# Small loads one per unit, and a rebuilt prologue with DMA transposes, in an attention and MLP kernel on one core

## Chip, core and metric

The kernel runs on one core of one Trainium2 chip. The metric is the time on the device in microseconds (us). The kernel before takes 1110.81 us (median of 3 runs, 1109.93 to 1113.89; with the fourth run, 1110.77). A "ratio" is the mean time of one kernel's runs over that of the kernel before in the same rounds, so it is not quite the ratio of the medians quoted beside it.

## The reference, cut to what matters

```python
xn = _layernorm(A_x)                       # 2048 x 1024, bf16
s = attention(xn, A_wqkv, A_wo)            # 32 heads of 32
h = gelu(layernorm(xn) @ w1 + b1)          # 1024 -> 3584
g = silu(h @ w2 + b2)                      # 3584 -> 1024
return A_x + s * g
```

## The kernel before

The program is straight-line code. A small scheduler on the host fixes the order of each engine's instructions. The attention runs in 512 "units" (8 head groups of 4 heads, 8 query blocks, 8 key pairs). Each unit has three parts:

- scores on TensorE (8 matmuls),
- two exps of 128x1024 on ScalarE,
- probabilities times V, with row sums, on TensorE ("PV", 16 matmuls).

Between scores and PV TensorE gets one "item" of other work, named by a letter of the plan. `a` is an MLP first layer item, `w` a second layer item, `q` a Q or K projection of later heads, `v` a V projection, `o` an output projection, and `.` is nothing. The first 8 units are the prologue. They make x normalised and transposed (`xnT`) and the first heads' Q, K and V, and have no items.

```python
def transp(tb):                      # 8 transposes of 128x128 on TensorE ...
    op("tensor", f, r=[("xnb", i), "ident"], w=[("b", bk)])
    op("scalar", copy of 128x1024 from PSUM to xnT[:, :, tb])     # ... and a copy on ScalarE
def mm4(e, outs, lhs, rhs, start, stop):      # one matmul as four tiles of 32 columns
    for j in range(4):
        e.matmul(outs(j), lhsT=lhs(j), rhs=rhs, tile_position=(0, 32 * j), ...)
def pair_kq(p):                      # mm4 for K, then Q: 64 matmuls; pair_v: 64 for V
    ...
def pro_unit(p):
    norm_pair(p + 1)                 # VectorE: statistics and x normalised, two tiles
    if p < 3: ynorm(p)               # VectorE: second normalisation, stored to DRAM
    if 0 < p < NP - 1: transp_pair(p + 1)
    pair_kq(p); pair_v(p)
    if p == 0: transp_pair(1)
# loads: wq 512 KB each, yTc one DMA transpose of 352x1024, wo one load of 2 MB,
# biases element by element:
op("gpsimd", lambda e: e.dma_start(b1T[:], B_b1.rearrange("(fb p) -> p fb", p=128)), ...)
... (cut)
```

All loads but those of the biases are issued by SyncE, in order. The MLP weights come in 336 loads of 256 KB.

The softmax here doesn't subtract the row's maximum and nothing guards it: scores larger than these inputs give would overflow.

Of the kernel before, what the change touches and what calls it, by code (L numbers as in the profile page):

```python
# [13 lines left out]
a v a a a q a q a v a v a a a q a a v a q a a v q a a v a a q a q a a v q a q a a a q q v a a q w3 w4 w3 w4 v w4 w2 w2 w2 a a v a q v v a q q a a a a a q a q a a q a a v a q a q q a a a v v a a a q v a a a a q q a a w3 v w3 w4 w4 w4 q v q v w2 v q w3 w3 a a a v v q a a a q a a q q a a a q q a v a q a v a a q a q a a a a v a a q a q v v v a a q q q v a q q a w3 q v q w5 q w4 w3 q w3 w4 w2 w4 a a a v v a a q a a q a q q v a a q a q v a q a a a a q a a a q a a v a a a a v a v a q a v q q w3 w4 v q w4 w4 w4 v w4 w3 w4 a a a q q a a a a v a v a a a a a v q a a v a a a q a a a v a a q q v a q q a a q a q q q a v w3 v w4 w4 q w4 w4 w4 w4 w4 a a a a q q a a q a a q a a a q a q q a a a a a a a a a a q q a a a a a q a q w2 w4 w3 w4 w2 w3 w5 o o o o o o o o o o o o w4 o o o o o o o o o o o o o o o o o o o o o o o o o o o . o o o o o o o . o o  # L14
# [153 lines left out]
def bass_recurrent_scan__mha_block__mixer_channel_mlp__prompt_kernel(  # L168
# [32 lines left out]
    t0 = 0  # L201
# [9 lines left out]
    with ExitStack() as st:  # L211
# [30 lines left out]
        gst = [sb(f"gst{i}", [128, CW], BF16) for i in range(2)]  # L242
        b1T = sb("b1T", [128, FB], F32)
# [10 lines left out]
        xnb = [hflat[:, i * D:(i + 1) * D] for i in range(4)]  # L254
# [23 lines left out]
        def load_wq(hp, which=(0, 1, 2)):  # L278
            for t3 in which:
                src = A_wqkv[:, t3 * D + hp * 256:t3 * D + (hp + 1) * 256].rearrange("(c p) n -> p c n", p=128)  # L280
                op("sync", lambda e, src=src, t3=t3: e.dma_start(wq[:, t3, :, :], src), w=[("wq", t3)], dma=f"wq{t3}", c=512)

        for tb in range(4):
            load_x(tb)
            if tb in (1, 3):
                load_wq(0, (1 if tb == 1 else 0,))
        load_x(4)
        load_x(5)
        load_wq(0, (2,))
        for tb in range(6, NT):  # L290
            load_x(tb)
# [4 lines left out]
        op("gpsimd", lambda e: e.dma_start(b1T[:], B_b1.rearrange("(fb p) -> p fb", p=128)), w=["b1"], dma="b1", c=256)  # L296
        op("gpsimd", lambda e: e.dma_start(b2h[:], B_b2.rearrange("(nb p) -> p nb", p=128)), w=["b2"], dma="b2", c=64)


# [8 lines left out]
        def rstd(b):  # L308
            lo, hi = 2 * b, 2 * b + 2
            L = lambda k: lnp[:, k, lo:hi]  # L310
            mvk = [("mv", t) for t in range(lo, hi)]
            op("vector", lambda e: e.tensor_scalar_add(L(0), mv[:, lo:hi, 1], EPS), r=mvk, w=[("l0", b)], c=169.0)
            op("gpsimd", lambda e: e.tensor_tensor(L(2), L(0), mhalf[:, 0:2], op=ALU.pow), r=[("l0", b), "mhalf"], w=[("l2", b)], c=708.0)  # L313

        def nbias(b):
            lo, hi = 2 * b, 2 * b + 2
            L = lambda k: lnp[:, k, lo:hi]
            mvk = [("mv", t) for t in range(lo, hi)]
            op("vector", lambda e: e.scalar_tensor_tensor(L(3), mv[:, lo:hi, 0], -1.0, L(2), op0=ALU.mult, op1=ALU.mult),
               r=mvk + [("l2", b)], w=[("l3", b)], c=107.0)  # L320

        def ycoef(b):
            lo, hi = 2 * b, 2 * b + 2
            L = lambda k: lnp[:, k, lo:hi]
            mvk = [("mv", t) for t in range(lo, hi)]
            op("gpsimd", lambda e: e.tensor_tensor(L(4), mv[:, lo:hi, 1], L(2), op=ALU.mult), r=mvk + [("l2", b)], w=[("l4", b)])
            op("gpsimd", lambda e: e.tensor_tensor(L(4), L(4), L(2), op=ALU.mult), r=[("l4", b), ("l2", b)], w=[("l4", b)])
            op("gpsimd", lambda e: e.tensor_scalar(L(4), L(4), 1.0, EPS, op0=ALU.mult, op1=ALU.add), r=[("l4", b)], w=[("l4", b)])
            op("gpsimd", lambda e: e.tensor_tensor(L(5), L(4), mhalf[:, 0:2], op=ALU.pow), r=[("l4", b), "mhalf"], w=[("l5", b)], c=760.0)
            op("gpsimd", lambda e: e.tensor_tensor(L(6), L(2), L(5), op=ALU.mult), r=[("l5", b), ("l2", b)], w=[("l6", b)])  # L330
            op("gpsimd", lambda e: e.tensor_tensor(L(7), L(3), L(5), op=ALU.mult), r=[("l5", b), ("l3", b)], w=[("l7", b)])

        def xnorm(tb):
            i = tb % 4
            op("vector", lambda e: e.tensor_scalar(xnb[i], xst[:, tb * D:(tb + 1) * D], lnp[:, 2, tb:tb + 1], lnp[:, 3, tb:tb + 1],  # L335
                                                   op0=ALU.mult, op1=ALU.add),
               r=[("xst", tb), ("l2", tb // 2), ("l3", tb // 2)], w=[("xnb", i)], c=545.0)
# [7 lines left out]
        pro_banks = [4, 5, 7]  # L345
        pbk = {"n": 0}
# [5 lines left out]
        def transp(tb):  # L352
            i, bk = tb % 4, pro_bank()
# [23 lines left out]
        def qk_item(hg, which, t0, n):  # L377
# [3 lines left out]
            def step(dc, bk):  # L381
                op("tensor", lambda e: mm4(e, lambda j: bankq(bk, j, 0, n),
                                           lambda j: wq[:, which, dc, co + 32 * j:co + 32 * j + 32],
                                           xnT[:, dc, t0:t0 + n], dc == 0, dc == DC - 1),
                   r=[("wq", which)] + [("xnT", t) for t in toks(t0, n)], w=[("b", bk)], c=("col", 1, n))
# [7 lines left out]
        def v_item(hp, tb):  # L393
            i2 = hp % 2

            def step(dc, bk):
                op("tensor", lambda e: mm4(e, lambda j: bankq(bk, j, 0, 256),
                                           lambda j: xnT[:, dc, tb * 128 + 32 * j:tb * 128 + 32 * j + 32],
                                           wq[:, 2, dc, :], dc == 0, dc == DC - 1),
                   r=[("wq", 2), ("xnT", tb)], w=[("b", bk)], c=("col", 1, 256))  # L400
# [77 lines left out]
        def load_y(c):  # L478
            t0, n = chunks[c]
            op("sync", lambda e: e.dma_start_transpose(yTc[:, :, 0:n], y_d[t0:t0 + n, :]),  # L480
               r=[("y", t) for t in toks(t0, n)], w=["yTc"], dma="yTc", c=1000)

        def w1_item(c, f):
# [8 lines left out]
            def step(dc, bk):  # L492
# [3 lines left out]
                   r=[("war", s, dc // 2), "yTc"], w=[("b", bk)], c=("col", 1, n))  # L496

            def fin(bk):
# [30 lines left out]
                def gate(i, xq, kq, fq):  # L529
                    op("vector", lambda e: e.scalar_tensor_tensor(hT[:, fq, 0:n], ut[:, i, 0:n], 1.0, xq[:, 0:n], op0=ALU.add, op1=ALU.mult),  # L530
                       r=[kus[i], kq], w=[("hT", fq)] + ([("xnb", i) for i in range(4)] if c == 0 else []), c=151 + 1.042 * n)
# [3 lines left out]
                if f == FB - 1 and c + 1 < NCH:  # L535
                    load_y(c + 1)
# [43 lines left out]
        def load_res(tb):  # L580
            i4 = tb % NTB
            op("sync", lambda e: e.dma_start(xres[i4], x2[tb * 128:(tb + 1) * 128, :]), w=[("xres", i4)], dma=f"rx{i4}", c=256,
               after=[tail["xfree"]])
            lo, hi = tb * 128, (tb + 1) * 128
# [5 lines left out]
        def wo_item(tb, k):  # L590
# [3 lines left out]
            def pre():  # L594
                if k == 0:
                    if tb == 0:
                        for t in range(NTB):
                            load_res(t)
                    elif tb + NTB - 1 < NT:
                        load_res(tb + NTB - 1)  # L600

            def step(hc, bk):
# [4 lines left out]
                   r=["wo", ("OT", hc, tb // 2)], w=[("b", bk)], c=("col", 1, n))  # L607

            def fin(bk):
# [5 lines left out]
                   r=[("b", bk), ("gres", i4)], w=[("ofin", f2)] + ([("wq", t) for t in range(3)] if m < 2 else []), c=165 + 1.042 * n)  # L615
# [10 lines left out]
        def pair_kq(p):  # L626
            t0, bk = 256 * p, pro_bank()

            def f(e):
                for which, off in ((1, 0), (0, 256)):  # L630
                    for dc in range(DC):
                        ins = mm4(e, lambda j: bankq(bk, j, off, off + 256), lambda j: wq[:, which, dc, 32 * j:32 * j + 32],
                                  xnT[:, dc, t0:t0 + 256], dc == 0, dc == DC - 1)
                return ins
            op("tensor", f, r=[("wq", 0), ("wq", 1), ("xnT", 2 * p), ("xnT", 2 * p + 1)], w=[("b", bk)], c=("col", 16, 256))
            for nm, dst, off in (("KT", KT, 0), ("QT", QT, 256)):
                op("scalar", lambda e, dst=dst, off=off: e.activation(dst[0][:, t0:t0 + 256], bank(bk, off, off + 256), ACT.Copy),
                   r=[("b", bk)], w=[(nm, 0, 2 * p), (nm, 0, 2 * p + 1)], c=263.0)

        def pair_v(p):  # L640
            bk = pro_bank()

            def f(e):
                for i in range(2):
                    t0 = (2 * p + i) * 128
                    for dc in range(DC):
                        ins = mm4(e, lambda j: bankq(bk, j, 256 * i, 256 * i + 256), lambda j: xnT[:, dc, t0 + 32 * j:t0 + 32 * j + 32],
                                  wq[:, 2, dc, :], dc == 0, dc == DC - 1)
                return ins
            op("tensor", f, r=[("wq", 2), ("xnT", 2 * p), ("xnT", 2 * p + 1)], w=[("b", bk)], c=("col", 16, 256))  # L650
# [3 lines left out]
        def norm_pair(p):  # L654

            more = p + 1 < NP
            if more and p >= 2:
                stat(2 * p + 2)
            nbias(p)
            xnorm(2 * p)  # L660
            xnorm(2 * p + 1)
            if more:
                if p < 2:
                    stat(2 * p + 2)
                stat(2 * p + 3)
                rstd(p + 1)
            ycoef(p)

        def transp_pair(p):
            transp(2 * p)  # L670
            transp(2 * p + 1)

        stat(0)
        stat(1)
        rstd(0)
        norm_pair(0)
        transp_pair(0)

        def pro_unit(p):
            if p + 1 < NP:  # L680
                norm_pair(p + 1)
            if p < 3:
                ynorm(p)
            if 0 < p < NP - 1:
                transp_pair(p + 1)
            pair_kq(p)
            pair_v(p)
            if p == 0:
                transp_pair(1)


# [12 lines left out]
        DU = NP  # L704
# [136 lines left out]
        while u < NU + LAG or state["qi"] < total or dq or act_tasks:  # L841
# [3 lines left out]
            elif u == NP:  # L845
# [98 lines left out]
```

## Time and profile before

| engine | busy us of 1108.7 | what it does |
|---|---|---|
| TensorE | 1082.7 | the limit over nearly the whole run |
| ScalarE | 1049.5 | exps, tanh; busy 59.9 of the 60 us from 65 to 125 us |
| VectorE | 630.4 | normalisation at first, then evictions and gelu |

First, the line of the page with each engine's busy time, share of the span and instructions.

```profile
PE 1082.7 (98%) x29952; PEld 706.5 (64%) x29952; DVE 630.4 (57%) x1415; ACT 1049.5 (95%) x1197; POOL 24.0 (2%) x64
```

Only 26 us of TensorE idle time exist. The TensorE timeline of the kernel before gives start, length, operation, count and, in brackets, the idle time before it and what ended it. In a line, `ps<-xnT,wq` names the tensor written (ps, in PSUM) and those read, `128*32` the rows and columns of the array in use, and `L366` the line of the kernel. It shows the beginning, the prologue unit 3, and the first unit after the prologue.

```profile
8.15 1.89 PE L357 MATMUL ps<-ident,hT 128*128 128x128 bf16 x16 [8.15 <-DVE hT L335]
11.50 3.61 PE L366 MATMUL ps<-xnT,wq 128*32 128x256 bf16 x64 [1.46 <-DMA wq<-in_A_wqkv_dram]
...
31.23 1.07 PE L357 MATMUL ps<-ident,hT 128*128 128x128 bf16 x16
32.23 1.93 PE L366 MATMUL ps<-xnT,wq 128*32 128x256 bf16 x64
33.99 1.92 PE L366 MATMUL ps<-wq,xnT 128*32 128x256 bf16 x64
35.84 0.40 PE L761 MATMUL ps<-QT,KT 32*128 32x256 bf16 x8
...
59.28 0.40 PE L761 MATMUL ps<-QT,KT 32*128 32x256 bf16 x8 [1.66 <-ACT P L773]
```

Differences of starts give the parts of a unit: transposes 1.00 us, K and Q 1.76, V 1.85. A unit takes 5.49 us, and nothing in it waits.

The waits of TensorE from 60 us on, in the kernel before (us in total, times, longest), are few; one of 0.2 us is left out:

```profile
PE ps L761 <- ACT P L773: 3.9, 13, 0.5
PE ps L366 <- issue: 2.9, 4, 1.4
PE ps L793 <- issue: 0.5, 1, 0.5
```

"issue" is idle time for which the profile shows no dependency. It sums to 3.4 us in five stalls. The longest is this one:

```profile
967.49 0.30 PE L366 MATMUL ps<-hT,war 128*32 128x288 bf16 x1 [1.41 <-issue]
```

### The profile page before, as it was taken

Reading aid. Unit: us, or ns where it says so; the run is one execution under the profiler, and the core shown is the slowest. Engines: PE = TensorE matmul, PEld = TensorE weight load, DVE = VectorE, ACT = ScalarE, POOL = GpSimd, SP = SyncE. Lnnn points to the kernel's source line nnn. Section 1 sums busy time; section 2 is a strip of 40 time slices with the busy share of each in tenths; the row PEclk is TensorE's granted clock in tenths of the full one; section 3 lists DMA queues with packets and bytes.
Section 4 is the critical chain, followed back from the end, with each engine's and each line's share of the span. In section 5 each row is a group of like instructions: output and inputs, shape, how many; then the busy total and the mean of one; then the engine's idle time right before and its main releaser. Section 6 shows DMA issues by size and latency. Waiting matters only on the chain.

```text
span 1108.7 us, 63340 instructions
## 1 busy us (share of the span) xinstructions
PE 1082.7 (98%) x29952; PEld 706.5 (64%) x29952; DVE 630.4 (57%) x1415; ACT 1049.5 (95%) x1197; POOL 24.0 (2%) x64
## 2 busy tenths in 40 slices
PE   6999999999999999999999999999999999999998
PEld 4866666666666666666666666666666666666665
DVE  8468762377742477652276852277743377624556
ACT  4899999899999999999999999999999999999994
POOL 4300000000000000000000000000000000000000
PEclk9999999999999999999999999999999999999999
DMA  9245255323353323333433334433234324557353
GB/s 237 71 145 174 89 146 153 114 79 108 99 150 98 89 80 114 110 87 88 130 108 92 115 76 126 144 111 108 80 104 118 111 81 144 159 155 156 96 136 108
DMA packets 202420, 129.93 MB, mean 117 GB/s; under 512 B 45488, under 2 KB 192944, under 8 KB 202160
## 3 DMA queue, kind: packets, MB, share of 16 engines
q1 hardware_dynamic: 197520, 125.86, 39.7%
q8 instruction: 234, 3.83, 1.4%
q0 software_dynamic: 4640, 0.02, 0.6%
q14 instruction: 26, 0.21, 0.1%
HBM read 104.87 MB, written 12.58 MB: 106 GB/s over the span
## 4 chain that ended last, share of the span: by engine, by line
PE 65%; ACT 32%; DVE 2%; issue 1%; DMA 0%; POOL 0%
PE ps L366 41%; ACT P L773 29%; PE ps L761 10%; PE ps L790 7%; PE ps L793 7%; ACT u L524 3%; DVE stats L303 1%; PE ps L357 1%; ACT thz L566 0%; DMA OT<-in_A_x_dram 0%; DVE hT L335 0%; DVE wq L614 0%; POOL lnp L313 0%; DVE mv L305 0%; DVE xb L507 0%
## 5 line engine op out<-in xcount | busy, mean ns | idle before, releaser
L773 ACT ACTIVATE P<-ps 128x1024 bf16<-128x1024 f32 x1024 | 970.0, 1069 | 18.1 <-PE ps L761 11.9
L793 PE MATMUL ps<-P,ones 128*32 128x256 bf16 x4096 | 257.7, 273 | 0.6 <-issue 0.5
L790 PE MATMUL ps<-P,VP 128*32 128x256 bf16 x4096 | 257.5, 273 | 0.0
L366 PE MATMUL ps<-hT,war 128*32 128x352 bf16 (+1 forms) x5376 | 226.1, 309 | 1.5 <-issue 1.4
L366 PE MATMUL ps<-yTc,war 128*32 128x352 bf16 (+1 forms) x5376 | 226.4, 309 | 0.4 <-issue 0.4
L761 PE MATMUL ps<-QT,KT 32*128 32x256 bf16 x4096 | 204.1, 273 | 7.6 <-ACT P L773 5.5
L366 PEld LDWEIGHTS ps<-hT,war 128*32 128x32 bf16 x5376 | 128.0, 96 | 76.2 <-issue 27.6
L366 PEld LDWEIGHTS ps<-yTc,war 128*32 128x32 bf16 x5376 | 127.5, 96 | 75.8 <-DVE xb L507 17.2
L562 DVE TENSOR_SCALAR zh<-ps,b2h 128x352 f32<-128x352 f32 (+1 forms) x48 | 27.5, 573 | 207.4 <-PE ps L366 207.4
L507 DVE TENSOR_SCALAR xb<-ps,b1T 128x352 f32<-128x352 f32 (+1 forms) x168 | 96.2, 573 | 78.5 <-PE ps L366 75.3
L761 PEld LDWEIGHTS ps<-QT,KT 32*128 32x128 bf16 x4096 | 61.0, 92 | 119.8 <-issue 65.7
L366 PE MATMUL ps<-xnT,wq 128*32 128x352 bf16 (+2 forms) x3200 | 130.0, 306 | 2.1 <-DMA wq<-in_A_wqkv_dram 1.5
L790 PEld LDWEIGHTS ps<-P,VP 128*32 128x32 bf16 x4096 | 110.4, 97 | 21.4 <-issue 1.7
L793 PEld LDWEIGHTS ps<-P,ones 128*32 128x32 bf16 x4096 | 110.5, 97 | 19.6 <-issue 1.1
L530 DVE SCALAR_TENSOR_TENSOR hT<-u,xb 128x352 bf16<-128x352 f32 (+1 forms) x168 | 83.8, 508 | 62.3 <-ACT u L524 62.2
L366 PEld LDWEIGHTS ps<-xnT,wq 128*32 128x32 bf16 x3200 | 77.5, 97 | 41.6 <-DVE xb L507 10.7
L517 DVE SCALAR_TENSOR_TENSOR u<-u,xb 128x352 f32<-128x352 f32 (+1 forms) x168 | 82.5, 509 | 1.9
L513 DVE TENSOR_TENSOR u<-xb 128x352 f32<-128x352 f32 (+1 forms) x168 | 82.5, 508 | 0.8
L524 ACT ACTIVATE u<-u 128x704 f32<-128x704 f32 (+1 forms) x84 | 69.9, 833 | 0.0
L366 PE MATMUL ps<-wq,xnT 128*32 128x256 bf16 x2048 | 66.6, 274 | 1.8 <-issue 1.1
L366 PE MATMUL ps<-xnT,OT 128*32 128x352 bf16 (+1 forms) x1536 | 62.9, 309 | 0.2 <-DVE wq L614 0.2
L366 PEld LDWEIGHTS ps<-wq,xnT 128*32 128x32 bf16 x2048 | 50.2, 96 | 14.0 <-DVE xb L507 5.5
(44 smaller groups left out, 435.5 us busy)
## 6 DMA issues: line engine op xcount, KB each, us to landing
war<-in_B_w_dram SPq DMA_DIRECT2D x336, 256.0 KB, 3.9
wq<-in_A_wqkv_dram SPq DMA_DIRECT2D x12, 512.0 KB, 5.3
OT<-in_A_x_dram SPq DMA_DIRECT2D x16, 256.0 KB, 7.7
y_scratch<-OT SPq DMA_DIRECT2D x16, 256.0 KB, 2.9
xnT<-in_A_x_dram SPq DMA_DIRECT2D x16, 256.0 KB, 3.8
out_dram<-wq SPq DMA_DIRECT2D x16, 256.0 KB, 2.0
gT_scratch<-gst SPq DMA_DIRECT2D x40, 88.0 KB, 1.7
xnT<-in_A_wo_dram SPq DMA_DIRECT2D x1, 2048.0 KB, 9.2
```

Source lines behind the costliest of these rows:

```text
L303: op("vector", lambda e, c=c: e.bn_stats(stats[:, tb, c, :], xt[:, c * 512:(c + 1) * 512]), r=[("xst", tb)], w=[("st", tb, c)], c=677.0)
L366: ins = e.matmul(outs(j), lhsT=lhs(j), rhs=rhs, start=start, stop=stop, tile_position=(0, 32 * j), skip_group_check=True)
L507: x0 = op("vector", lambda e: e.tensor_scalar(xb[:, 0:n], bank(bk, 0, n), b1T[:, f:f + 1], None, op0=ALU.add), r=[("b", bk), "b1"], w=[kx] ...
L513: x = op("vector", lambda e: e.tensor_tensor(ub[:, 0:n], xb[:, 0:n], xb[:, 0:n], op=ALU.mult), r=[kx], w=[ku], c=151 + 1.042 * n)
L517: x = op("vector", lambda e: e.scalar_tensor_tensor(ub[:, 0:n], ub[:, 0:n], 1.0 / 0.044715, xb[:, 0:n], op0=ALU.add, op1=ALU.mult), r=[kx, ...
L524: x = op("scalar", lambda e: e.activation(ut[:, :, 0:n], ut[:, :, 0:n], ACT.Tanh, scale=0.7978845608028654 * 0.044715), r=kus, w=kus, c=48 ...
L530: op("vector", lambda e: e.scalar_tensor_tensor(hT[:, fq, 0:n], ut[:, i, 0:n], 1.0, xq[:, 0:n], op0=ALU.add, op1=ALU.mult), r=[kus[i], kq] ...
L562: x0 = op("vector", lambda e: e.tensor_scalar(zh[:, 0:n], bank(bk, 0, n), 0.25, b2h[:, nb:nb + 1], op0=ALU.mult, op1=ALU.add), r=[("b", bk ...
L761: ins = e.matmul(bank(bks[j], kh * 256, (kh + 1) * 256), lhsT=KT[i2][32 * j:32 * j + 32, k0:k0 + 128], rhs=QT[i2][32 * j:32 * j + 32, qb * ...
L773: op("scalar", lambda e, p=p, sl=sl: e.activation(pb[:, 2 * p:2 * p + 2, :, :].rearrange("p a b q -> p (a b q)"), ps[:, sl * 1024:(sl + 1) ...
L790: e.matmul(bankq(ACC, j, 0, QW), lhsT=VP[vp][:, kb, vo + 32 * j:vo + 32 * j + 32], rhs=pb[:, j, kh, :], start=first, stop=False, tile_posi ...
L793: ins = e.matmul(bankq(ACC, j, QW, 2 * QW), lhsT=ones[:, 0:32], rhs=pb[:, j, kh, :], start=False, stop=last, tile_position=(0, 32 * j), sk ...
```

## The change

The change intends to shorten the prologue and to keep large loads from coming in bursts. Its parts:

1. x tiles 8 to 15 are transposed by DMA from SBUF, not by TensorE and ScalarE.
2. The prologue's projections are plain 128-column matmuls, not four tiles.
3. The biases come as rows, and one TensorE transpose turns them.
4. Loads at the start are reordered, tile 0 is normalised before tile 1's statistics, and three y normalisations move to ScalarE.
5. Items begin in unit 7 (`q` moves there from unit 13, which becomes `.`).
6. In the steady part wq comes in parts of 128 KB, the y transpose in four, wo in eight with the x tiles of the residual between them, about one per unit.

```diff
-a v a a a q a q a v ...
+q a v a a a . a q a v ...
+        def wq_part():
+            hp, t3, lo = wq_due.pop(0)
+            load_wq(hp, (t3,), lo, lo + 2)
-        op("gpsimd", lambda e: e.dma_start(b1T[:], B_b1.rearrange("(fb p) -> p fb", p=128)), ...)
+            op("sync", lambda e: e.dma_start(brow[0:FB, :], B_b1.rearrange("(fb p) -> fb p", p=128)), ...)
+            if tb >= TDMA:                                   # TDMA = 8
+                op("sync", lambda e: e.dma_start_transpose(xnT[:, :, tb * 128:(tb + 1) * 128], xnb[i]), ...)
+                return
-                        ins = mm4(e, lambda j: bankq(bk, j, off, off + 256), ...
+                        ins = e.matmul(bank(bk, off, off + 256), lhsT=wq[:, which, dc, 0:128], rhs=xnT[:, dc, t0:t0 + 256], ...
-                    load_y(c + 1)
+                    for s4 in range(4):
+                        sp_tasks[cur["u"] + 2 + 2 * s4].append((load_y, c + 1, s4))
-                    op("sync", lambda e: e.dma_start(wo_sb, A_wo.rearrange("(c p) n -> p c n", p=128)), ... c=2048, ...)
+                    for h in range(HG):
+                        sp_tasks[u + 1 + 2 * h].append((load_wo, h))
-            if u >= NP and state["qi"] < total:
+            if u >= NP - 1 and state["qi"] < total:
... (cut)
```

## The prediction

> **What bounds the kernel now.** Busy table: TensorE 1082.7 of 1108.7 us, ScalarE 1049.5. Only 26 us of TensorE idle time exist. The TensorE timeline places it: 8.15 us before the first transpose, 1.46 and 0.64 for wq loads, 1.66 at 57.6 us (the first unit after the prologue waits for an exp), and issue stalls of 0.62, 0.33, 0.77, 0.52, 0.38, 1.41. The 1.41 at 966 us falls while the 2 MB wo load is in flight. The prologue ends at 59.28 us (scores of unit 8). Its units take 5.49 us, all TensorE: transposes 1.00, K/Q 1.76, V 1.85, scores 0.33, PV 0.55; ScalarE works 4.8 of them.
>
> **What changes, costed.**
> 1. Transposes of tiles 8 to 15 leave TensorE (four pairs of 1.00 us) and ScalarE (1.83). Those units then need about 4.4 us. A DMA transpose of this size from DRAM (gT) costs SyncE 1.17 us to issue and lands after 4.9; I take the same from SBUF, an estimate.
> 2. Untiled projections: no gain per column. A tiled round takes 1.76/16 = 110 ns; an untiled 256-column matmul should too, because full weights already keep up with 62 ns per transpose. Saved: three of four instructions and one mode switch per unit. The Trainium skill ("TensorEngine Tiling (Array Packing)", Key Properties) says a change of tiling mode drains TensorE; the trace shows about 0.1 us (PV 0.55 for four rounds of 0.11).
> 3. Start: the bias loads, 4640 tiny packets, 0.6% of 16 engines' span (6.6 us of all engines) in the first 20 us, go. V's weights move ahead of x4; K need not wait for Q's weights; tile 0 is normalised before tile 1's statistics. Scores of unit 0 at 15.5, not 18.6.
> 4. VectorE loses three y normalisations; a pair takes it 4.13 us, ahead of 4.4 us units.
> 5. The q item in unit 7 fills the wait at the prologue's end; the "." falls where ScalarE is the limit (full in 70 to 120), so it costs nothing.
> 6. Small parts: the Trainium skill ("Runtime: NRT & Kernel Launch", Instruction fetch mechanics) says instructions are fetched by DMA in 16 KiB blocks; bursts may hold these up. I expect 2 of the 3.4 us of issue stalls after the prologue back. The next heads' weights arrive many units before use: no new waits.
>
> **Sum.** Scores of unit 0 at 15.5; units 1 to 3 about 5.4 each, ending at 32; up to 1.5 wait for the first DMA-transposed pair; four units of 4.4; 2.5 with the q item: scores of unit 8 near 52, 7 us sooner, all on the critical path because ScalarE and TensorE are both full after it. With 2 us from stalls and a little from less switching: 1110.8 - 9.5 = about 1101 us. Range 1096.5 to 1106.5. Faster by over 2%: 0.02; within: 0.96; slower: 0.02.
>
> **What would show it.** Timeline: untiled K/Q about 1.75 us; no transposes from unit 3 on; units 4 to 7 at 4.4 us; unit 8 at 50 to 54. No wait over 2 us on DMA-transposed xnT. Issue stalls after 60 us under 1.5 us in sum.
>
> **What would make it wrong.** DMA transposes from SBUF much slower than from DRAM, or SyncE clogged by them, so that units 4 to 7 wait (gain under 4 us); VectorE waiting for later x tiles; issue stalls with another cause; the gain at the start given back where ScalarE limits.

## The result, and the profile after

The changed kernel takes 1102.42 us (median of 4 runs, 1100.28 to 1102.9). The ratio is 0.9916, with a 95% interval of 0.9893 to 0.9939. A repeat with five runs gave 1103.17 us (ratio 0.993, 0.9918 to 0.9942). The first profile is of the fastest of its four runs (1100.28 us), which will matter.

The page's busy line after:

```profile
PE 1077.4 (98%) x29121; PEld 701.4 (64%) x29121; DVE 629.1 (57%) x1413; ACT 1044.4 (95%) x1194; POOL 20.0 (2%) x63
```

TensorE's timeline after shows the beginning, unit 2, the units 4 and 5 without transposes, and the first unit after the prologue:

```profile
7.45 1.89 PE L389 MATMUL ps<-ident,hT 128*128 128x128 bf16 x16 [7.45 <-DVE hT L359]
10.61 3.57 PE L675 MATMUL ps<-xnT,wq 128*128 128x256 bf16 x16 [1.27 <-ACT xnT L392]
...
26.11 1.92 PE L691 MATMUL ps<-wq,xnT 128*128 128x256 bf16 x16 [0.56 <-ACT QT L681]
...
33.33 1.92 PE L675 MATMUL ps<-xnT,wq 128*128 128x256 bf16 x16
35.08 1.91 PE L691 MATMUL ps<-wq,xnT 128*128 128x256 bf16 x16
36.92 0.40 PE L824 MATMUL ps<-QT,KT 32*128 32x256 bf16 x8
...
37.80 1.92 PE L675 MATMUL ps<-xnT,wq 128*128 128x256 bf16 x16
...
53.07 0.40 PE L824 MATMUL ps<-QT,KT 32*128 32x256 bf16 x8 [0.45 <-ACT P L836]
```

A unit without transposes takes 4.47 us (33.33 to 37.80). K and Q take 1.75 us for 16 matmuls, as they took for 64. The view of DMA issues (count, median us to landing) has the new transposes. They land in 2.8 us; those from DRAM, later in the run, take 4.8:

```profile
xnT<-gT_scratch SPq DMA_TRANSPOSE x16, 4.8
xnT<-hT SPq DMA_TRANSPOSE x8, 2.8
```

Both kernels have the same 512 units in the same order, so they can be laid side by side. Below is the start of each unit's scores matmuls, read from the timelines.

| unit | before, us | after, us | difference |
|---|---|---|---|
| 0 | 18.61 | 16.86 | -1.75 |
| 3 | 35.84 | 32.45 | -3.39 |
| 6 | 52.30 | 46.01 | -6.29 |
| 8 | 59.28 | 53.07 | -6.21 |
| 10 | 63.10 | 57.79 | -5.31 |
| 14 | 71.45 | 65.72 | -5.73 |
| 100 | 251.44 | 246.16 | -5.28 |
| 188 | 434.13 | 427.35 | -6.78 |
| 300 | 665.17 | 656.68 | -8.49 |
| 440 | 945.00 | 936.14 | -8.86 |
| 450 | 968.16 | 957.24 | -10.92 |
| 511 | 1090.75 | 1080.46 | -10.29 |

The prologue wins 6.2 us, and 0.9 of them go again in units 8 and 9. In unit 8 (0.27 us) the first MLP item waits for one of its weight loads. In unit 9 (0.63 us) the first V item waits for its weights, which are issued in four parts behind the y transposes. Later the gain grows in steps. Five of these (at units 105, 186, 297, 444 and 450) together make 4.6 us, and each sits at one of the five issue stalls of the kernel before. TensorE's waits from 60 us on have no long issue stall after (two other lines, of 0.3 and 0.2 us, are left out):

```profile
PE ps L824 <- ACT P L836: 3.8, 14, 0.5
PE ps L398 <- issue: 0.4, 2, 0.2
```

### The profile page after: what moved, and what is told of

Same layout as the page of the kernel before. It is cut to its first block, busy times and chain, and to the rows that moved or that the text cites. A ratio compares the mean times of both kernels' runs of the same rounds, so it can differ in the third digit from the quotient of the medians.

```text
span 1098.4 us, 61752 instructions
## 1 busy us (share of the span) xinstructions
PE 1077.4 (98%) x29121; PEld 701.4 (64%) x29121; DVE 629.1 (57%) x1413; ACT 1044.4 (95%) x1194; POOL 20.0 (2%) x63
## 4 chain that ended last, share of the span: by engine, by line
PE 56%; ACT 38%; DVE 3%; SPq 1%; DMA 1%; issue 0%; POOL 0%
PE ps L398 35%; ACT P L836 35%; PE ps L824 9%; PE ps L856 6%; PE ps L853 6%; ACT u L558 3%; DVE stats L326 2%; DVE hT L359 1%; SPq L514 0%; DMA wq<-in_A_wqkv_dram 0%; ACT thz L601 0%; DVE mv L328 0%; SPq L382 0%; DMA OT<-in_A_x_dram 0%; DMA y_scratch<-OT 0%
## 5 line engine op out<-in xcount | busy, mean ns | idle before, releaser
L398 PE MATMUL ps<-xnT,wq 128*32 128x352 bf16 (+1 forms) x2688 | 112.7, 309 | 0.0
L398 PEld LDWEIGHTS ps<-xnT,wq 128*32 128x32 bf16 x2688 | 63.9, 96 | 36.8 <-DVE xb L541 10.2
L398 PE MATMUL ps<-wq,xnT 128*32 128x256 bf16 x1536 | 51.3, 274 | 0.4 <-DMA wq<-in_A_wqkv_dram 0.3
L398 PEld LDWEIGHTS ps<-xnT,OT 128*32 128x32 bf16 x1536 | 37.4, 97 | 20.0 <-DVE wq L658 8.1
```

The costliest lines, as they stand in the source:

```text
L398: ins = e.matmul(outs(j), lhsT=lhs(j), rhs=rhs, start=start, stop=stop, tile_position=(0, 32 * j), skip_group_check=True)
```

## Experiments

Two theories stood for the late steps. Theory A: bursts of loads delay the fetch of TensorE's instructions. Rival R: the stalls are chance, or follow from where the fetched blocks happen to fall in the program. Of the prologue's parts, 1, 2, 3 and 5 were undone alone; part 4, the order of loads and normalisations at the start, was not. Edits are against the changed kernel unless said otherwise, and times are medians.

| run | runs | us, median (range) | ratio to before |
|---|---|---|---|
| changed kernel, first | 4 | 1102.42 (1100.28 to 1102.9) | 0.9916 |
| rep_after | 5 | 1103.17 (1102.8 to 1104.91) | 0.993 |
| tiled | 6 | 1106.71 (1104.81 to 1110.51) | 0.9964 |
| whole | 5 | 1105.92 (1103.54 to 1107.58) | 0.9949 |
| tdma16 | 4 | 1107.83 (1106.85 to 1111.8) | 0.9975 |
| late_item | 4 | 1102.67 (1102.0 to 1103.89) | 0.992 |
| bias_old | 4 | 1102.54 (1101.46 to 1104.72) | 0.9923 |
| best_a | 4 | 1101.66 (1101.45 to 1103.06) | 0.9915 |
| pace2 | 6 | 1101.01 (1100.33 to 1102.06) | 0.991 |
| pace3 | 6 | 1101.15 (1099.7 to 1103.22) | 0.9909 |
| best_pace2 | 5 | 1100.08 (1099.25 to 1100.28) | 0.9898 |
| best_pace3 | 5 | 1100.28 (1098.54 to 1100.76) | 0.9897 |

The kernel before had medians of 1110.77 to 1111.29 us in all four sets of rounds. The record numbers the chips of the last three sets 2, 12 and 15, so the ratio is the safer measure where runs of different sets are compared.

### Both kernels once more: rep_before, rep_after

No edit.

> The kernel before, unchanged, profiled once more. Theory A (the issue stalls of TensorE come from load bursts that hold up its instruction fetch): stalls of about the same size come again, 3 to 4 us after 60 us, and the largest again within 10 us after the 2 MB wo load is issued (near 966 us). Rival R (the stalls are chance): other places, other sum, perhaps under 1.5 us. Scores of unit 8 at 59.3 in both.

> The changed kernel, unchanged. Its four runs lay between 1100.3 and 1102.9 and the profiled one was the fastest. Theory A: no issue stall of 0.3 us or more again, unit 8 again 6.2 us and unit 511 about 10 us ahead of before. Rival R: stalls of 1 to 3 us appear in this execution. Ratio to before 0.990 to 0.993.

The repeat of the kernel before took 1113.46 us. It had seven issue stalls of 0.25 us or more after 60 us, 5.53 us in sum, against five and 3.41 us in its first profile. Three are at the same units as before (105, 297 and 450), but the one at unit 105 grew from 0.33 to 1.71 us and others are new. So the places partly recur and the sizes vary. The repeat of the changed kernel had four stalls of 0.25 us or more, 1.93 us in sum. The view of waits from 60 us on counts the shorter ones too (2.5 us in all):

```profile
PE ps L856 <- issue: 1.1, 2, 0.9
PE ps L398 <- issue: 1.1, 4, 0.4
PE ps L853 <- issue: 0.3, 1, 0.3
```

The first profile, with no stall of that size, was therefore a lucky one, and my expectation of no stall of 0.3 us failed. It was lucky at the start too: in the repeats unit 0's scores start at 19.05 us before and 17.91 after, and unit 8's at 59.86 and 54.12, so the prologue wins 5.7 us there and not 6.2. Of the 2.5 us between the two profiled runs of the changed kernel, 1.05 were lost before unit 0's scores and 1.93 are such stalls; a part came back elsewhere.

What a stall is can be read in the trace's DMA records. One queue (the page calls it instruction, q8) moved 234 blocks of 16 KB before and 228 after; the page's lines (packets, MB, share of the 16 engines), before and after:

```profile
q8 instruction: 234, 3.83, 1.4%
q8 instruction: 228, 3.74, 1.4%
```

TensorE's 29952 matmuls and 29952 weight loads are 234 times 256 instructions, so this queue carries TensorE's program. The records give the start of every block. Around ten of the 23 stalls of 0.25 us or more after 60 us in five profiles:

```
kernel      stall ends   last block landed before it:   gap to the block before   stall ends after landing
before        260.95     started 258.70                       7.08                     1.32
before        428.99     started 426.60                       7.57                     1.43
before        658.88     started 656.46                       5.49                     1.48
before        952.86     started 950.45                       7.77                     1.45
before        967.49     started 964.91                       7.24                     1.60
rep_before    263.51     started 261.13                       8.62                     1.45
rep_before    969.57     started 966.95                       7.46                     1.61
whole         963.54     started 960.96                       7.12                     1.46
tdma16        261.79     started 259.36                       8.47                     1.47
best_a        256.49     started 254.12                       8.10                     1.43
```

Blocks follow each other at 4.5 us in the median. Before 20 of the 23 stalls a block started 5.2 to 10.7 us after the last; before three (two in whole, one in tdma16) the gap was an ordinary 4.2 to 4.7 us. All 35 such stalls in the fourteen profiles, 0.26 to 1.71 us long, end 1.15 to 1.63 us after a block has landed. With a block every 4.5 us, chance would put about one in nine there (an estimate, 0.48 of 4.5 us), so what ends the stall is the block. The late blocks are not slow in moving (about 1 us, as others); they start late. Nor is TensorE merely slower at using up its program: at the start of each of these 35 blocks it had already begun 20 to 224 more instructions, counted against the blocks fetched so far, than at the start of the median block.

What makes a block late is less clear. In the two profiles of the kernel before, the DMA engines were 0.65 busy in the 6 us ahead of the blocks that came over 6.5 us after the last (12 and 11 of them), and 0.44 in the median ahead of ordinary ones (0.87 from 419 to 426 us, ahead of the stall at 428.99). But one in five ordinary blocks came through with over 0.6 as well. So busy engines go with late blocks and are not enough. The Trainium skill ("Runtime: NRT & Kernel Launch", Instruction fetch mechanics) says that each engine fetches 16 KiB blocks over its own DMA queue and that the cost is mostly hidden. The block size agrees. Most fetches are hidden here too: in the two profiles of the kernel before, five and seven of 234 blocks came with a stall of 0.25 us or more.

### Whole loads again: whole

```diff
-                        wq_due.extend((hp, t3, lo) for t3 in reversed(which) for lo in range(0, DC, 2))
+                        load_wq(hp, which)
-                        for s4 in range(4): sp_tasks[...].append((load_y, c + 1, s4))
+                        load_y(c + 1)                        # one transpose
-                    for h in range(HG): sp_tasks[u + 1 + 2 * h].append((load_wo, h))
+                    op("sync", ... wo_sb in one load of 2 MB ...)
```

> The changed kernel with whole loads again in the steady part: wq 512 KB at once, the y transpose in one, wo 2 MB at once. Theory A: issue stalls come back, about 1.5 us near unit 450 (wo) and 0.5 to 1 us at one to three other places, 2 to 4 us in all; the V weights for the item in unit 9 come 0.5 to 0.9 us earlier, so units 9 and 10 win that. Net 1.5 to 3.5 us slower than the changed kernel. Rival R (stalls by chance or by where the 16 KiB blocks of instructions fall): no more stalls than in the changed kernel, and 0.5 to 1 us faster than it.

It is 2.75 us slower than the changed kernel in the same rounds (1105.92 to 1103.17), though the ranges overlap (intervals of the ratio 0.9936 to 0.9961 and 0.9918 to 0.9942). The issue stalls of 0.25 us or more sum to 3.91 us against 1.93, with 0.99 us at unit 451 while wo loads. Units 8 and 9 won 0.27 and 0.07 us over the first profile (0.47 and 0.37 over the repeat), less than expected: in unit 9 TensorE still waited 0.48 us for V's weights. The time and the stalls are theory A's expectation. One thing is not: the gaps of over 6.5 us between blocks, five, are no more than in the changed kernel (five and four). The issue stalls from 60 us on, short ones included:

```profile
PE ps L855 <- issue: 1.8, 2, 1.0
PE ps L852 <- issue: 1.0, 1, 1.0
PE ps L398 <- issue: 0.7, 1, 0.7
PE ps L823 <- issue: 0.7, 2, 0.4
```

### At most two or three weight loads in flight: pace2, pace3

```diff
-            op("sync", ..., w=[("war", s, q)], dma=f"war{s}{q}", c=256)
+            op("sync", ..., w=[("war", s, q)], dma=f"war{next(nwar) % 2}", c=256)    # pace3: % 3
```

Loads that share a semaphore wait for each other, so this bounds the weight loads in flight: in the traces at most two and three, against up to seven in the changed kernel. Sizes, bytes and TensorE's instructions stay. A load that waits also holds up what stands behind it in SyncE's queue.

> The changed kernel with one more edit: the 336 MLP weight loads of 256 KB share two semaphores in turn, so that a load waits until the last but one has landed and no more than two are ever in flight; sizes, bytes and TensorE's instructions stay as they are. Theory A (a block of TensorE's instructions that falls due while many loads are queued starts late, and TensorE runs dry): gaps between block fetches over 6.5 us (4 to 5 in the changed kernel, 11 to 12 in the kernel before, between 60 and 1050 us) become 0 to 2, issue stalls after 60 us under 0.5 us in sum, the time 0.5 to 2 us below the changed kernel's 1102.4 to 1103.2 and its spread narrower. Rival R (stalls come from where the blocks fall, not from the loads' number in flight): as many gaps and stalls as before. If loads then come too late: waits for war of over 1 us.

> As the run with two loads in flight, but with three. Theory A: between the changed kernel and the run with two: 1 to 4 gaps over 6.5 us, stalls under 1 us in sum, no waits for war.

| profile | block gaps over 6.5 us (60 to 1050 us) | issue stalls of 0.25 us or more after 60 us |
|---|---|---|
| before, rep_before | 12, 11 | 3.41, 5.53 us |
| changed, rep_after | 5, 4 | 0, 1.93 us |
| whole | 5 | 3.91 us |
| tiled, tdma16, late_item, bias_old, best_a | 9, 6, 7, 8, 6 | 0.60, 2.83, 2.68, 0.64, 1.35 us |
| pace3, best_pace3 | 3, 3 | 0.75, 0 us |
| pace2, best_pace2 | 1, 1 | 0, 0 us |

The four profiles with bounded loads have 1 to 3 long gaps and at most 0.75 us of stalls; the eight others with the change have 4 to 9 gaps and up to 3.91 us. (best_pace3 has one stall of 0.89 us at 58.84 us, just before the count begins.) This speaks for theory A and against R: TensorE's instructions, and so the places where blocks end, are the same in pace2, pace3, whole and the changed kernel. The number of long gaps alone does not give the stalls: five gaps went with 0 us in the first profile and with 3.91 us in whole. How a load holds up a block stays open.

In time the gain is not resolved. pace2 comes out 1.4 to 2.2 us below the two medians of the changed kernel, but it was not run in the same rounds, and the intervals of the ratio overlap (0.9894 to 0.9926 against 0.9893 to 0.9939 and 0.9918 to 0.9942). Its waits from 60 us on show the price, one late weight load:

```profile
PE ps L399 <- DMA war<-in_B_w_dram: 0.7, 1, 0.7
PE ps L399 <- issue: 0.2, 1, 0.2
```

### All transposes on TensorE: tdma16

```diff
-        TDMA = 8
+        TDMA = NT
```

> The changed kernel with all sixteen tiles transposed on TensorE again. Theory A (the prologue is TensorE's time, so the four pairs of transposes at 1.00 us are worth their full time): units 3 to 6 take 5.4 to 5.5 us instead of 4.5, scores of unit 8 at 57 to 57.5, 4 us later than in the changed kernel, and the whole 4 us slower, ratio to before 0.996 to 0.997. Rival R3 (the prologue then hides behind VectorE's normalisation or is made up later, where ScalarE limits): unit 8 later by under 2.5 us or the end later by under 2.5 us.

Scores of unit 8 started at 58.08 us, 5.0 us later than after (5.1 us when both are counted from unit 0, which leaves out the scatter at the start), and the kernel was 4.7 to 5.4 us slower than the two medians. So DMA transposes are the largest single part, and their whole time counts. It is more than 4.0 us because two more units now have ScalarE behind, with an idle 0.57 us each, the unit 2 pattern:

```profile
32.12 1.92 PE L691 MATMUL ps<-wq,xnT 128*128 128x256 bf16 x16 [0.57 <-ACT QT L681]
38.23 1.92 PE L691 MATMUL ps<-wq,xnT 128*128 128x256 bf16 x16 [0.57 <-ACT QT L681]
```

### Tiled projections again: tiled

```diff
-                        ins = e.matmul(bank(bk, off, off + 256), lhsT=wq[:, which, dc, 0:128], rhs=xnT[:, dc, t0:t0 + 256], ...
+                        ins = mm4(e, lambda j: bankq(bk, j, off, off + 256), lambda j: wq[:, which, dc, 32 * j:32 * j + 32], ...
```

The V projection was changed alike.

> The changed kernel with the prologue's projections tiled four ways again, as before the change. My reading of the trace: an untiled 256-column matmul takes 110 ns as a tiled round does, so only mode switches count. Units 3 to 7, which hold no transposes any more, should take 4.37 us (unit 7 of before) and not 4.47, units 0 to 2 0.1 us longer: scores of unit 8 about 0.3 us earlier, time unchanged within 1 us. The prediction's claim (untiling saves a switch in every unit) would have it 0.8 us later. Rival R2 (three times more matmul instructions cost time by themselves): unit 8 later by over 1 us, and issue stalls come back.

My reading of the switches was right and beside the point. Unit 3 to unit 4 took 4.37 us, 0.1 less than untiled. The Trainium skill ("TensorEngine Tiling (Array Packing)", Key Properties) says that a change of tiling mode drains the array. In units without transposes, untiling adds a change to the order PV (tiled), K (full), V (full), scores (row), and the price here is 0.1 us. But three issue stalls (0.49, 0.36 and 0.39 us) came back in the prologue: up to 53 us TensorE fetched nine blocks of instructions, as before the change, where the changed kernel needs four. Each of the three ended 1.25 to 1.33 us after a block had landed. Scores of unit 8 were 1.4 us later. This is rival R2's picture, in one profile.

A further 3.4 us went in unit 8, where the first MLP item waited for weights whose load was issued behind the y transposes:

```profile
57.78 0.48 PE L398 MATMUL ps<-yTc,war 128*32 128x352 bf16 x4 [2.19 <-DMA war<-in_B_w_dram]
```

A view of windows (length; busy time and count of TensorE, its weight loads, VectorE, ScalarE and GpSimd; granted clock, DMA share, GB/s) shows what that wait set off. The clock was at half for 3.41 us (57.74 to 61.15 in the clock records), inside the second window:

```profile
54.00:57.70 3.70, 1.29 (x32) 0.46 (x24) 0.98 (x2) 2.35 (x3) 0.00 (x0) 1.00 0.93 161
57.70:61.20 3.50, 3.35 (x52) 1.39 (x56) 1.47 (x4) 0.35 (x1) 0.00 (x0) 0.51 0.92 280
```

Why SyncE reached that load 3.9 us later than in the changed kernel (53.90 against 50.02) was not settled. Two weight loads before it took 3.08 us to issue instead of 0.96.

### Items one unit later: late_item

```diff
-        DU = NP - 1
+        DU = NP                 # and the old plan, items from u >= NP
```

> The changed kernel with the first item in unit 8 again and the old order of items. The prediction's step 5 says that the q item in unit 7 fills a wait of 1.66 us, so its place in unit 13 is won. My reading of the two traces: the wait at the end of the prologue comes back (about 1.7 us idle before scores of unit 8) with the start of unit 8 unchanged at 53 us, because the item just fills it, and units 8 to 13 then take one more item: where ScalarE limits, an item less saves 0.4 us (unit 13 took 1.65 us instead of 2.07). So 0.4 us slower at unit 14, 0 to 1 us at the end. If the whole item counted it would be 1.3 us.

The wait before unit 8 came back at 1.64 us, and unit 8 started at 53.54 us. It lost 0.42 us at units 13 to 14, as expected, and 1.0 us more in units 8 and 9 (0.5 us against the repeat of the changed kernel), where it waited for MLP weights and then for V's:

```profile
53.54 0.40 PE L824 MATMUL ps<-QT,KT 32*128 32x256 bf16 x8 [1.64 <-ACT P L836]
57.88 0.40 PE L398 MATMUL ps<-wq,xnT 128*32 128x256 bf16 x8 [0.58 <-DMA wq<-in_A_wqkv_dram]
```

The time (1102.67 us) does not differ from the changed kernel's. What this part is worth in time is not resolved.

### Biases element by element again: bias_old

```diff
+        op("gpsimd", lambda e: e.dma_start(b1T[:], B_b1.rearrange("(fb p) -> p fb", p=128)), w=["b1"], dma="b1", c=256)
-            if p == 3: load_bias()
-            if p == 3 + 2: turn_bias()
... (cut: the same for the second bias)
```

> The changed kernel with the biases loaded in 2-byte pieces by GpSimd's queue again, as before. The prediction put the removal into the gain at the start. Reading of the traces: in 4 to 9 us the loads move 200 to 250 GB/s with the small pieces and 370 to 400 without. K waits for the transposed x, not for its weights, and Q and V come behind, so scores of unit 0 stay at 16.9 to 17.2; x of tiles 4 and 5 lands 1 to 2 us later, VectorE waits for it, and unit 2 or 3 gets later by 0.5 to 1.5 us. Rival: no effect at unit 8 (under 0.3 us), so the bias change only tidies up.

Scores of unit 0 stayed (16.92 us). Unit 1 was 1.7 us later, because tile 4 came late to VectorE:

```profile
20.82 1.08 PE L392 MATMUL ps<-ident,hT 128*128 128x128 bf16 x16 [1.65 <-DVE hT L362]
```

At unit 8 it was 1.6 us behind the first profile (1.55 when both are counted from unit 0), at unit 511 1.25. The medians do not show it (1102.54 against 1102.42 and 1103.17); this profile had only 0.64 us of stalls. So the part is worth about 1.5 us where it acts, as this one trace shows, and its worth in time is below what these rounds resolve.

### Four edits at the start: best_a, best_pace2, best_pace3

```diff
+        op("tensor", warm, ...)                   # 54 transposes of ident into an unused bank, from 1.4 us
+        for q in range(4): load_sub(0, q)         # first MLP weights behind the x loads
-            if p >= 2: ynorm_pro(p - 2)
+            if p >= 3: ynorm_pro(p - 3)
+                        if qi == 0: load_wq(hp, which)     # first V weights in one load
-q a v a a a .
+q a a v a a .
... (cut)
```

> The changed kernel with four more edits at the start: 54 transposes of the identity into an unused bank while TensorE waits for the first tile (the first 16 projection matmuls took 3.4 us, twice as long as later ones; if that is a cold clock, they take 1.8); the first four MLP weight loads issued behind the x loads; the V weights of the next heads in one load and their item one unit later; the three y normalisations on ScalarE one unit later. Expected: scores of unit 0 at 15.5 to 16.0 instead of 16.9, the wait of 0.56 us in unit 2 gone, unit 8 0.8 to 1.5 us earlier (VectorE's 4.13 us per pair sets the limit from unit 4 on), and the 0.9 us lost in units 8 to 10 not lost. About 2 us faster than the changed kernel, 0.991 or lower to before. If the slow first matmuls are not the clock, unit 0 stays at 16.9.

> The four edits at the start (warm TensorE, early MLP weights, V weights whole and later, y normalisation later) and two loads in flight. The start wins 1.1 us by unit 8 and 1.6 by unit 10 over the changed kernel's profile; without the stalls at units 11, 32 and 105 of the run without pacing nothing takes that back. Expected 1099.5 to 1101, 0.990 to before; if stalls do not depend on the loads in flight, 1101.7 as without pacing.

> The four edits at the start and three loads in flight: 1099.5 to 1101.5. Should two in flight bring late weights, this one is the faster of the two.

The edit that busies TensorE early did what it should. The 16 matmuls of K and Q of unit 0 now span 1.91 us, as in later units, instead of 3.57, and unit 0's scores started at 15.66 us:

```profile
1.37 5.16 PE L731 MATMUL ps<-ident 128*128 128x128 bf16 x54 [1.37 <-DVE ident L309]
...
10.24 1.91 PE L675 MATMUL ps<-xnT,wq 128*128 128x256 bf16 x16 [1.31 <-ACT xnT L392]
```

The Trainium skill ("TensorE: Matmul & The Clock Gate", Part 1) says that an idle array runs at half clock until about 3.4 us of work have passed. The first clock record of this trace, at full clock, begins at 5.55 us, 4.2 us after the early work began, that of the changed kernel at 14.26 us, and the span fell from 3.57 to 1.91 us. Unit 2's wait was gone, and unit 8 came at 52.00 us, 1.1 us sooner than after. Then, in unit 10, the V item waited 0.46 us for its weights, a stall of 0.64 us for instructions came in the same item, and two more stalls followed at units 32 and 105. They took it back: 1101.66 us, not clearly better.

With two loads in flight the same edits gave 1100.08 us (1099.25 to 1100.28); the fastest of the nine runs of the changed kernel took 1100.28. That is 0.9 us below pace2 in the same rounds, with overlapping intervals of the ratio (0.9882 to 0.9913 and 0.9894 to 0.9926). With three in flight the ratio is 0.9897, which cannot be told from it. In the profile with two in flight the lead at the start is gone by unit 11, because the V item waits 1.15 us for its weights, and near the end TensorE waits 1.26 us for MLP weights. So the order of these few loads still has something to give.

## Why the prediction was right, and where its steps were not

The forecast was 1101 us (1096.5 to 1106.5); measured were 1102.42 and 1103.17. The sum held, while several terms did not. The large term, the transposes, was right; that the sum came so close is in part luck, because errors of opposite sign met: the start and unit 2 lost time against it, units 1 and 3 won some.

- **Transposes (step 1): right in size and place.** Units without them take 4.47 us (predicted 4.4), and undoing it costs 4.7 to 5.4 us. The landing time, taken as 4.9 us from the DRAM case, was 2.8. The wait of up to 1.5 us did not come.
- **Untiling (step 2): the reason was wrong.** "One mode switch per unit" is not saved in units without transposes; one is added (4.47 against 4.37 us). "Three of four instructions" was named but given no price, and there the worth lay: four blocks fetched instead of nine, and no stalls in the prologue. In the experiment 1.4 us by unit 8 hung on it.
- **Start (step 3): half of it.** Scores of unit 0 came 1.75 us sooner (1.1 in the repeats), not 3.1. The sum took K and Q at 1.76 us there, although the trace before showed 3.6 for the first. The cold clock costs about 1.6 us. The bias change acted, but in unit 1, not unit 0.
- **Sum of units 1 to 3:** "5.4 each" was wrong in unit 1 (5.0), unit 2 (6.1, ScalarE's y normalisation ahead of the Q copy, a clash I had not looked for) and unit 3 (4.5, it has no transposes any more, as the prediction itself says two lines below). These errors nearly cancel: unit 8 at 53.07, inside the 50 to 54 named, and at 54.12, just outside, in the repeat.
- **"No new waits" for the next heads' weights (step 6): wrong for the first V item.** It gave back 0.6 us in unit 9, and a late MLP weight load 0.3 us in unit 8.
- **Stalls (step 6): right in kind.** Predicted 2 us back. The first profile had 3.0 of the 3.4 us idle gone and 4.6 us of steps, the repeat still had 1.93 us of stalls, above the 1.5 us named, and undoing the small parts cost 2.75 us in time. That the stalls end with the landing of a block is shown; that many loads in flight delay blocks is supported by the pacing runs; how they do so is open.
- **q item in unit 7 (step 5):** it does fill the wait. Its gain shows in the trace (0.42 us at unit 13) but not in the times.

Undone alone, the transposes cost 4.7 to 5.4 us, untiling 3.5 and the small loads 2.75. That is more than the whole gain of 8.1 to 8.4 us, so these costs are not shares of it.

## What to carry to other kernels

Where one engine is 98% busy and issues tens of thousands of instructions, look at idle time without a dependency, and compare it with the starts of that engine's instruction fetches: bounding the loads in flight nearly removed such stalls in the profiles here without moving any of TensorE's work, though the gain in time was too small to resolve. Lay two profiles side by side by unit, not only by total, because a sum can hit while its terms are off, and repeat the profile of both kernels, since one execution may lack the very stalls under study. When work moves to an engine or a queue with slack, check what stands next to it in that queue (the Q copy behind y normalisation, the V weights behind the y transposes).

## What the Trainium skill lacked or had wrong

- "Runtime: NRT & Kernel Launch", Instruction fetch mechanics, calls the cost of a block boundary mostly hidden and has no word on loads delaying fetches. Here five and seven of 234 blocks came with a stall of 0.25 us or more before the change, 3.4 and 5.5 us in sum, 1.71 us the longest. With two weight loads in flight the gaps over 6.5 us fell to 1, from 5 and 4 in the changed kernel.
- "DMA: Bandwidth & Descriptors" (Queues, rings and completion order) says that each DMA engine takes turns between queues after a packet. Whether the instruction queue gets such turns the runs cannot tell: ahead of the stalls listed above, blocks started 1 to 4 us later than the median spacing, and which step held them up was not shown.
- "TensorE: Matmul & The Clock Gate", Part 1, gives an idle window of about 3.4 us before the clock halves. In the run tiled the clock record shows half clock for 3.41 us from 57.74 us, though TensorE had been busy for 1.12 of the 3.41 us before (the longest idle time was 2.19 us), so the window was not wholly idle. Also, the first clock record of the changed kernel begins at 14.26 us, and the view of windows shows 1.00 before it, where K and Q of unit 0 ran at 210 ns per matmul (16 from 10.61 to 13.97 us) instead of 110; no page says that a clock column can be blind there.
- "DMA: Bandwidth & Descriptors", DMA Transpose, has no time to landing for a transpose from SBUF. Here 128x1024 bf16 landed in 2.8 us (2.7 to 4.4) and cost SyncE about 1.27 us to issue.
